# Softcap attention and two feed-forward blocks on one core: sums on fewer or narrower products, and six weight units in plain f32

## The chip, the cores and the metric

The kernel runs on one core of a Trainium2 chip. Its time is the device time of one execution in microseconds; the number for a kernel is the median over several runs. The engines are TensorE (PE in the profile, PEld for its weight loads), VectorE (DVE), ScalarE (ACT), GpSimd (POOL) and SyncE (SP), which issues most DMAs. ScalarE issues some too. TensorE writes into PSUM, the others work between PSUM and SBUF.

## The reference, cut to what matters

```python
def _attn_ref(q, k, v, cap):                 # 4 batches, 12 heads, 448 rows, 64 wide
    scores = 1/sqrt(64) * q @ k^T
    scores = cap * tanh(scores / cap)
    attn = exp(scores - max(scores))
    attn = attn / (sum(attn) + 1e-9)
    return attn @ v

x = attention, heads side by side: (4 * 448, 768)
h = x @ w_in                                 # 768 -> 2048
g = h if h >= 1, 0 if h <= -1, else (h + 1)^2 / 4
y = g @ w_out                                # 2048 -> 768
m = max(y @ w1, y @ w2, y @ w3)              # 768 -> 768
out = m @ w_o2                               # 768 -> 768
```

Everything is f32. The weights arrive as 64-bit words and are turned into f32 on the chip.

## The kernel before

The work is cut by batch (four of 448 tokens) and, in attention, by pairs of heads (six a batch). Tokens lie on the free axis throughout, so the scores of a pair come out transposed, keys on partitions: four chunks of 112 keys, each a tile `t` of 112 x 2 x 448. A row's maximum and sum therefore run across partitions and chunks. For the maximum VectorE joins the four chunks into `mx` and GpSimd reduces over partitions into `mb` (`partition_all_reduce`, L453). VectorE subtracts `mb` from the chunks and ScalarE takes exp.

The sum is taken in one of three ways, by batch. In batch 0 TensorE multiplies each of the four chunks by a 112 x 64 block of ones, for two heads (`total`, L485). In batch 1 it does so with 32 columns of ones and half of the 448 tokens a product, four products side by side a chunk (`total4`, L499). In batches 2 and 3 (`POOLED`) VectorE adds the four chunks into one tile `se` with three additions, and GpSimd reduces it over partitions into `sb` (L534). For all pairs but the last of batch 0, the sums are then gathered by a DMA into a small tile `rc`, turned over there by VectorE, and spread by two more DMAs over a tile `rs`; for the last pair VectorE takes reciprocals of the full tile. Meanwhile TensorE weighs `v` with the chunks into `ps_a` (L619). `xf` is `ps_a` times `rs`.

The feed-forward layers need more precision than a single pass of the type fp32r gives. Each operand is split into a high part and the rest: a copy to fp32r (ScalarE or VectorE) and a subtraction (VectorE). A *part* is one 128 x 128 block of weights against one 128 x 448 tile, in three products: high by high, high by rest, rest by high (L667 to L669). Weights come in 64 units of up to six parts: units 0 to 15 are w_in, 16 to 39 w_out, 40 to 57 w1 to w3, 58 to 63 w_o2. In batch 0 a unit is loaded as 64-bit words (`raw`), converted by VectorE, ScalarE and VectorE (L333, L340, L346) into `wf`, stored to DRAM as f32 and split into `w`; later batches load the stored f32 and split it again. `raw` has three buffers, `wf` and `w` four each.

All operations of the kernel are recorded first, with a due time (`want`), a cost for each engine that can do them, and their tiles. `Plan.run` then places them one by one by due time and by when an engine and a buffer are free, and the engines' programs are emitted in the order that comes out. So a cost or a due time in the table of an operation moves other operations too. Two rules matter here: where two kinds of TensorE work follow each other the plan adds `TURN`, and when GpSimd starts an operation the plan books VectorE for `SHARE` us as well (L136 to L139). The attention of batch b + 1 is spread over the feed-forward pass of batch b; that of batch 0 comes first, with nothing beside it.

```python
    SHARE = 1.4
    FOURS, POOLED = (1,), (2, 3)
    ep = op({"P": 2.95}, reduce_sum, begin + 10 + 7 * gap, [sm], [se], [sb])
    PART, SCORE, STEP, SUM = 0.609, 0.8, 0.755, 0.39
```

Of the kernel before, what the change touches and what calls it, by code (L numbers as in the profile page):

```python
# [14 lines left out]
ALU = mybir.AluOpType  # L15
# [5 lines left out]
class Plan:  # L21
# [43 lines left out]
    def run(self):  # L65
# [39 lines left out]
        while left:  # L105
            moved = True
            while moved:
# [9 lines left out]
                for o in ready:  # L117
# [16 lines left out]
                        c += self.TURN if o.kind != last else 0.0  # L134
                        last = o.kind
                    if e == "P":  # L136
                        free_at["D"] = max(free_at["D"], t) + self.SHARE
                        heapq.heappush(events, (free_at["D"], serial, None))
                        serial += 1  # L139
                    if e == "Q":  # L140
# [54 lines left out]
def kernel(  # L195
# [23 lines left out]
    NF = w_in.shape[0]  # L219
    NM = w123.shape[1]  # L220
    WU = w_in.shape[2]
    FOURS, POOLED = (1,), (2, 3)

    def pool(name, bufs, **kw):
        return ctx.enter_context(tc.tile_pool(name=name, bufs=bufs, **kw))
# [144 lines left out]
    def weights(b, i, want):  # L370

        n = width[i]
        wf, got = (fetch_first if b == 0 else fetch_again)(i, want)
        w = buf("w", "w", [P, 2, WU], F32R)
        hi = op(
            c_copy(n / 1000),
            lambda e: copy(e, w.tile[:, 0, :n], wf.tile[:, :n]),
            want - 9, [got], [wf], [w],
        )
        lo = op(  # L380
            c_tt(n / 1000),
            lambda e: tt(
                e, w.tile[:, 1, :n], wf.tile[:, :n], f32(w.tile[:, 0, :n]), ALU.subtract
            ),
            want - 8, [got, hi], [wf, w],
        )
        return w, [hi, lo]


    def attention(b, i, begin, last):  # L390
# [113 lines left out]
            return fn  # L504

        w = begin + 9 + 6 * gap
        if fours or first:
            g = Group(NCH)
            sums = [
                op({"T": SUM if fours else STEP}, (total4 if fours else total)(t[c], g),  # L510
                   w + 0.1 * c, [exps[c]], [t[c], pr], [pr] if c == 0 else [],
                   "sums" if fours else "columns")
                for c in range(NCH)
            ]
            for c in range(1, NCH):
                sums[c].deps.append(sums[0])
        else:
            se = unit("se", rows=C)
            sm = op(
                c_tt(2 * KS),  # L520
                lambda e: tt(e, se.tile, t[0].tile, t[1].tile, ALU.add),
                w, exps[:2], [t[0], t[1]], [se],
            )
            for c in range(2, NCH):
                sm = op(
                    c_tt(2 * KS),
                    lambda e, c=c: tt(e, se.tile, se.tile, t[c].tile, ALU.add),
                    w + 0.1, [sm, exps[c]], [se, t[c]],
                )
            if pooled:  # L530
                sb = unit("sb", rows=C)

                def reduce_sum(e):
                    nc.gpsimd.partition_all_reduce(  # L534
                        out_ap=sb.tile.rearrange("p h s -> p (h s)"),
                        in_ap=se.tile.rearrange("p h s -> p (h s)"),
                        channels=C, reduce_op=bass.bass_isa.ReduceOp.add,
                    )

                ep = op({"P": 2.95}, reduce_sum, begin + 10 + 7 * gap, [sm], [se], [sb])  # L540
            else:
                sums = [op(
                    {"T": STEP}, total(se, Group(1)), begin + 10.9 + 8 * gap, [sm], [se],
                    [pr], "columns",
                )]
        w = begin + 10 + 8.2 * gap

        cols = S // 2 if fours else S
# [14 lines left out]
        if small:  # L563
# [5 lines left out]
            def gather(e):  # L569
                if pooled:  # L570
                    src = sb.tile[0:1].rearrange("p h (c q) -> p (h c) q", q=C)
                else:
                    step = 32 if fours else D
                    src = rs.tile[0:P:step, :cols].rearrange("p (c q) -> p c q", q=C)
                nc.scalar.dma_start(out=rc.tile, in_=src)

            def spread(e):
                nc.sync.dma_start(out=back, in_=rc.tile)
# [6 lines left out]
                    )  # L585

            src = sb if pooled else rs
            r = op({"A": 0.6}, gather, w + 0.05, [ep], [src], [rc])
            r = op({"S": 3.0 if first else 5.0}, lambda e: None, w + 0.06, [r], [rc, src])

            def turn_over(e):
# [23 lines left out]
        def weigh(c):  # L615
# [10 lines left out]


        avs = [op(
            {"T": STEP}, weigh(0), w, [vl] + (exps[:1] if first else exps + ([] if pooled else sums)),
            [t[0], vt], [pa], "columns",  # L630
        )]
        for c in range(1, NCH):
# [15 lines left out]
            lambda e: tt(e, x.tile[:, 1], xf.tile, f32(x.tile[:, 0]), ALU.subtract),  # L648
            w + 1, [a, hi], [xf, x],
        )  # L650
        return x, [hi, lo]


    def sl(m):
# [1 line left out]

    def parts(pos, want, w, srcs, first, count, ps, g, take):

        wt, wops = w
        done = []  # L660
        for j in range(count):
            a, aops = srcs[first + j]

            def fn(e, j=j, a=a):
                start, stop = g.flags()
                wh, wl = wt.tile[:, 0][:, sl(j)], wt.tile[:, 1][:, sl(j)]
                nc.tensor.matmul(ps.tile[:, :S], wh, a.tile[:, 0], start=start, stop=False)  # L667
                nc.tensor.matmul(ps.tile[:, :S], wh, a.tile[:, 1], start=False, stop=False)  # L668
                nc.tensor.matmul(ps.tile[:, :S], wl, a.tile[:, 0], start=False, stop=stop)  # L669

            o = op(
                {"T": PART}, fn, want(pos + j), [*aops, *wops], [wt, a, ps],
                [ps] if take and j == 0 else [], "layer",
            )
            done.append(o)
        return done
# [176 lines left out]
```

## Time and profile before

| what | us or share |
|---|---|
| median of 3 runs | 1052.28 (1052.06 to 1053.23) |
| profiled execution / its span | 1049.13 / 1047.3 |
| TensorE busy | 1027.1 (98%), 5472 records |
| VectorE busy | 812.3 (78%) |
| ScalarE busy | 508.2 (49%) |
| GpSimd busy | 154.2 (15%), 36 reductions |
| HBM read and written | 131.89 and 27.61 MB |

The busy shares over the span, in 40 slices of 26 us (each digit in tenths, 9 is 90% or more):

```
PE   7988999999999999999999999999999999999998
DVE  5999999898994889868877589777788578655552
ACT  6887996674571856423523377525235144200101
POOL 2321012011010122132222031231221200000000
DMA  7339879889885332444234423335432432234331
```

The first three slices are the attention of batch 0. Then come four feed-forward passes of some 240 us each, the last without attention beside it and so shorter. A product with f32 operands is shown as two records, since it is issued in two; an fp32r product is one record. Products are pipelined: the duration shown of one overlaps the next, and the time that one takes out of TensorE is read from start to start. The page's time of the profiled execution is that of one execution; the median comes from others.

### The profile page before, as it was taken

Reading aid. Unit: us, or ns where it says so; the run is one execution under the profiler, and the core shown is the slowest. Engines: PE = TensorE matmul, PEld = TensorE weight load, DVE = VectorE, ACT = ScalarE, POOL = GpSimd, SP = SyncE. Lnnn points to the kernel's source line nnn. Section 1 sums busy time; section 2 is a strip of 40 time slices with the busy share of each in tenths; the row PEclk is TensorE's granted clock in tenths of the full one; section 3 lists DMA queues with packets and bytes.
Section 4 is the critical chain, followed back from the end, with each engine's and each line's share of the span. In section 5 each row is a group of like instructions: output and inputs, shape, how many; then the busy total and the mean of one; then the engine's idle time right before and its main releaser. Section 6 shows DMA issues by size and latency. Waiting matters only on the chain.

```text
span 1047.3 us, 14331 instructions
## 1 busy us (share of the span) xinstructions
PE 1027.1 (98%) x5472; PEld 813.3 (78%) x5472; DVE 812.3 (78%) x1066; ACT 508.2 (49%) x738; POOL 154.2 (15%) x40
## 2 busy tenths in 40 slices
PE   7988999999999999999999999999999999999998
PEld 2237787787888878878877888788788799999997
DVE  5999999898994889868877589777788578655552
ACT  6887996674571856423523377525235144200101
POOL 2321012011010122132222031231221200000000
PEclk9999999999999999999999999999999999999999
DMA  7339879889885332444234423335432432234331
GB/s 162 123 105 295 280 226 295 290 299 302 285 290 187 99 116 68 119 136 148 96 106 132 146 91 92 108 99 157 126 107 84 143 117 95 91 115 136 106 106 53
DMA packets 66783, 160.53 MB, mean 153 GB/s; under 512 B 8218, under 2 KB 25754, under 8 KB 66714
## 3 DMA queue, kind: packets, MB, share of 16 engines
q1 hardware_dynamic: 66256, 159.53, 48.2%
q8 instruction: 43, 0.70, 0.3%
q14 instruction: 26, 0.21, 0.1%
q10 hardware_dynamic: 458, 0.08, 0.0%
HBM read 131.89 MB, written 27.61 MB: 152 GB/s over the span
## 4 chain that ended last, share of the span: by engine, by line
PE 79%; DVE 7%; DMA 4%; ACT 3%; issue 3%; POOL 3%; SPq 1%; ACTq 0%; POOLq 0%; DVEq 0%
PE ps_m L667 23%; PE ps_m L669 22%; PE ps_m L668 22%; PE ps_s L425 5%; PE ps_a L619 5%; DVE t L257 2%; POOL mb L453 2%; POOL sb L534 1%; DVE mx L257 1%; DMA qk<-in_qk 1%; DVE w L257 1%; PE ps_r L499 1%; ACT t L471 1%; DVE h L750 1%; DMA wf<-w 1%
## 5 line engine op out<-in xcount | busy, mean ns | idle before, releaser
L257 DVE TENSOR_TENSOR w<-wf,w 128x768 fp32r<-128x768 f32 (+1 forms) x256 | 257.1, 1006 | 8.1 <-ACT w L252 4.5
L667 PE MATMUL ps_m<-y,w 128*128 128x448 f32 x432 | 160.4, 371 | 0.0
L254 DVE CAST w<-wf 128x768 fp32r<-128x768 f32 (+1 forms) x120 | 62.5, 521 | 125.2 <-PE ps_m L669 118.7
L668 PE MATMUL ps_m<-y,w 128*128 128x448 f32 x432 | 158.3, 366 | 0.0
L669 PE MATMUL ps_m<-y,w 128*128 128x448 f32 x432 | 158.3, 366 | 0.0
L453 POOL PARTITION_ALL_REDUCE mb<-mx x24 | 79.3, 3306 | 532.7 <-DVE mx L257 424.0
L669 PE MATMUL ps_m<-x,w 128*128 128x448 f32 x384 | 141.4, 368 | 2.9 <-DVE w L257 2.9
L252 ACT ACTIVATE w<-wf 128x768 fp32r<-128x768 f32 (+1 forms) x136 | 101.9, 752 | 86.3 <-PE ps_m L669 60.7
L667 PE MATMUL ps_m<-x,w 128*128 128x448 f32 x384 | 142.8, 372 | 0.0
L667 PE MATMUL ps_m<-g,w 128*128 128x448 f32 x384 | 142.5, 371 | 0.0
L668 PE MATMUL ps_m<-x,w 128*128 128x448 f32 x384 | 141.1, 367 | 0.0
L669 PE MATMUL ps_m<-g,w 128*128 128x448 f32 x384 | 140.5, 366 | 0.0
L668 PE MATMUL ps_m<-g,w 128*128 128x448 f32 x384 | 140.5, 366 | 0.0
L432 ACT ACTIVATE t<-ps_s,qscale 112x896 f32<-112x896 f32 x96 | 92.2, 1003 | 41.9 <-PE ps_s L425 41.9
L471 ACT ACTIVATE t<-t,cap_sb 112x896 f32<-112x896 f32 x96 | 96.5, 1037 | 23.8 <-DVE t L257 23.5
L257 DVE TENSOR_TENSOR t<-t,mb 112x896 f32<-112x896 f32 x96 | 100.1, 1080 | 6.7 <-POOL mb L453 6.7
L667 PEld LDWEIGHTS ps_m<-y,w 128*128 128x128 f32 x432 | 81.1, 188 | 20.3 <-issue 13.4
L425 PE MATMUL ps_s<-qk 64*48 64x448 f32 (+1 forms) x768 | 88.1, 562 | 6.8 <-DMA qk<-in_qk 4.5
L534 POOL PARTITION_ALL_REDUCE sb<-se x12 | 74.7, 6223 | 130.6 <-DVE se L257 118.4
L667 PEld LDWEIGHTS ps_m<-g,w 128*128 128x128 f32 x384 | 72.1, 188 | 18.8 <-issue 10.6
L669 PEld LDWEIGHTS ps_m<-y,w 128*128 128x128 f32 x432 | 81.1, 188 | 7.1
L668 PEld LDWEIGHTS ps_m<-y,w 128*128 128x128 f32 x432 | 81.2, 188 | 6.9
(60 smaller groups left out, 1464.5 us busy)
## 6 DMA issues: line engine op xcount, KB each, us to landing
wf<-w SPq DMA_DIRECT2D x120, 384.0 KB
wf<-w SPq DMA_DIRECT2D x72, 256.0 KB
w<-wf SPq DMA_DIRECT2D x40, 384.0 KB
raw<-in_w SPq DMA_DIRECT2D x18, 768.0 KB
raw<-in_w_in SPq DMA_DIRECT2D x16, 768.0 KB
raw<-in_w_out SPq DMA_DIRECT2D x24, 512.0 KB
qk<-in_qk SPq DMA_DIRECT2D x48, 224.0 KB
w<-wf SPq DMA_DIRECT2D x24, 256.0 KB
```

What stands on the lines that cost most here:

```text
L252: nc.scalar.activation(out=out_, in_=in_, func=AF.Copy)
L254: nc.vector.tensor_copy(out_, in_)
L257: nc.vector.tensor_tensor(out=out_, in0=a, in1=b, op=o)
L425: nc.tensor.matmul(ps.tile[k : k + n, j, :S], qkt.tile[o, 1, c * C + k : c * C + k + n], qkt.tile[o, 0], start=True, stop=True,)
L432: nc.scalar.activation(out=t[c].tile, in_=ps.tile[:C, :, :S], func=AF.Tanh, scale=qscale[:C])
L453: nc.gpsimd.partition_all_reduce(out_ap=mb.tile.rearrange("p h s -> p (h s)"), in_ap=mx.tile.rearrange("p h s -> p (h s)"), channels=C, re ...
L471: lambda e, c=c: nc.scalar.activation(out=t[c].tile, in_=t[c].tile, func=AF.Exp, scale=cap_sb[:C]),
L534: nc.gpsimd.partition_all_reduce(out_ap=sb.tile.rearrange("p h s -> p (h s)"), in_ap=se.tile.rearrange("p h s -> p (h s)"), channels=C, re ...
L619: nc.tensor.matmul(pa.tile[j * D : (j + 1) * D, :S], vt.tile[:, j, c], t[c].tile[:, j], start=start, stop=stop,)
L667: nc.tensor.matmul(ps.tile[:, :S], wh, a.tile[:, 0], start=start, stop=False)
L668: nc.tensor.matmul(ps.tile[:, :S], wh, a.tile[:, 1], start=False, stop=False)
L669: nc.tensor.matmul(ps.tile[:, :S], wl, a.tile[:, 0], start=False, stop=stop)
```

## The change

Four things are changed.

1. The sums of batch 0 (all pairs but the last) are taken by `total4`, as four products of 32 columns side by side a chunk, instead of two of 64.
2. In batch 1 VectorE first adds the chunks in twos (`se` of chunks 0 and 1, `se` of 2 and 3), and TensorE sums two tiles a pair instead of four. They fall due later than before, next to the weighing products.
3. For batches 2 and 3 the plan's cost of GpSimd's sum goes from 2.95 to 6.1, and the time booked on VectorE beside a GpSimd operation grows with that operation's cost (1.4 for 3 us). The DMA that gathers these sums is issued by SyncE instead of ScalarE.
4. The first six units of w_in are not split in batch 0: their parts are one f32 product each, of `wf` and `xf`.

```diff
-                        free_at["D"] = max(free_at["D"], t) + self.SHARE
+                        free_at["D"] = max(free_at["D"], t) + self.SHARE * c / 3
...
-    FOURS, POOLED = (1,), (2, 3)
+    PLAIN = 6
+    ADDED, FOURS, POOLED = (0, 2, 3, 3), (0, 1), (2, 3)
...
         wf, got = (fetch_first if b == 0 else fetch_again)(i, want)
+        if b == 0 and i < PLAIN:
+            return wf, [got], True
         w = buf("w", "w", [P, 2, WU], F32R)
...
-        return w, [hi, lo]
+        return w, [hi, lo], False
...
+        if ADDED[b] == 0:
+            srcs = list(zip(t, exps))
+        elif ADDED[b] == 2:
+            srcs = []
+            for c in (0, 2):
+                se = unit("se", rows=C)
+                srcs.append((se, add(t[c], t[c + 1], se, w, exps[c : c + 2])))
         else:
             se = unit("se", rows=C)
+            sm = add(t[0], t[1], se, w, exps[:2])
             for c in range(2, NCH):
+                sm = add(se, t[c], se, w + 0.1, [sm, exps[c]])
+            srcs = [(se, sm)]
...
-                ep = op({"P": 2.95}, reduce_sum, begin + 10 + 7 * gap, [sm], [se], [sb])
+            ep = op({"P": 6.1}, reduce_sum, begin + 10 + 7 * gap, [sm], [se], [sb])
+        else:
+            g = Group(len(srcs))
+            sums = [
+                op({"T": SUM if fours else STEP}, (total4 if fours else total)(x, g),
+                   (w if first else begin + 10.9 + 8 * gap) + 0.1 * c, [d], [x, pr],
+                   [pr] if c == 0 else [], "sums" if fours else "columns")
+                for c, (x, d) in enumerate(srcs)
+            ]
...
-                nc.scalar.dma_start(out=rc.tile, in_=src)
+                (nc.sync if pooled else nc.scalar).dma_start(out=rc.tile, in_=src)
...
-            r = op({"A": 0.6}, gather, w + 0.05, [ep], [src], [rc])
+            r = op({"Q": 0.1} if pooled else {"A": 0.6}, gather, w + 0.05, [ep], [src], [rc])
...
+            if plain:
+                a, aop = srcs[first + j][2:]
+                aops = [aop]
...
+                if plain:
+                    nc.tensor.matmul(
+                        ps.tile[:, :S], wt.tile[:, sl(j)], a.tile, start=start, stop=stop
+                    )
+                    return
...
-                {"T": PART}, fn, want(pos + j), [*aops, *wops], [wt, a, ps],
-                [ps] if take and j == 0 else [], "layer",
+                {"T": 0.755 if plain else PART}, fn, want(pos + j), [*aops, *wops],
+                [wt, a, ps], [ps] if take and j == 0 else [], "plain" if plain else "layer",
```

What this does to the engines' orders is shown at three places. In the rows, `x_...` and `xf_...` are tiles of batch 0's six pairs, and numbers tell buffers apart; they are other numbers after than before.

Order A, TensorE, from the last pair of batch 0's attention (`ps_r`, `ps_a`) into the first layer (`ps_m`). Before:

```order
L485 MATMUL ps_r_660<-t_577,ones_90 64x448 x2
L619 MATMUL ps_a_665<-t_577,v_489 64x448 x2
L667 MATMUL ps_m_699<-x_451,w_650 128x448
L668 MATMUL ps_m_699<-x_451,w_650 128x448
L669 MATMUL ps_m_699<-x_451,w_650 128x448
L667 MATMUL ps_m_699<-x_522,w_650 128x448
```

After:

```order
L677 MATMUL ps_m_695<-xf_562,wf_683 128x448
L490 MATMUL ps_r_700<-t_543,ones_90 64x448 x2
L625 MATMUL ps_a_705<-t_543,v_513 64x448 x2
L490 MATMUL ps_r_700<-t_574,ones_90 64x448 x2
L625 MATMUL ps_a_705<-t_574,v_513 64x448 x2
L677 MATMUL ps_m_695<-xf_637,wf_683 128x448
L677 MATMUL ps_m_695<-xf_691,wf_683 128x448
L677 MATMUL ps_m_749<-xf_482,wf_718 128x448
L677 MATMUL ps_m_695<-xf_747,wf_683 128x448
```

Each part is one product now; two of them (the first of unit 0, with `xf_482`, stands four rows above) come among pair 5's products, and after those come three parts that need no late `xf`, then one with pair 4's (`xf_747`), two more of unit 1, and the one with pair 5's.

Order B, TensorE, the sums (`ps_r`) and weighing products (`ps_a`) of batch 1's first pair, in units 5 to 7. Before:

```order
L499 MATMUL ps_r_949<-t_580,ones_90 32x224 x4
L499 MATMUL ps_r_949<-t_608,ones_90 32x224 x4
L499 MATMUL ps_r_949<-t_622,ones_90 32x224 x4
...
L499 MATMUL ps_r_949<-t_635,ones_90 32x224 x4
...
L619 MATMUL ps_a_1046<-t_580,v_569 64x448 x2
```

After:

```order
L504 MATMUL ps_r_964<-se_923,ones_90 32x224 x4
L504 MATMUL ps_r_964<-se_933,ones_90 32x224 x4
L625 MATMUL ps_a_982<-t_600,v_615 64x448 x2
L625 MATMUL ps_a_982<-t_623,v_615 64x448 x2
L625 MATMUL ps_a_982<-t_625,v_615 64x448 x2
L625 MATMUL ps_a_982<-t_633,v_615 64x448 x2
```

The sums are half as many and stand right ahead of the weighing products, with no layer product between.

Order C, VectorE, at the end of w1 to w3 in batch 1: `se` are the additions for GpSimd's sum of batch 2's last pair, `top` the maximum over the three layers' PSUM tiles, `w` a weight unit's second half, `m` the second half of the last tile of the next layer's input. Before:

```order
L257 TENSOR_TENSOR se_4938<-t_4806,t_4814 112x896
L257 TENSOR_TENSOR top_4918<-ps_m_4910,top_4918 128x448
L257 TENSOR_TENSOR se_4938<-se_4938,t_4831 112x896
L257 TENSOR_TENSOR se_4938<-se_4938,t_4836 112x896
L257 TENSOR_TENSOR w_4946<-wf_4809,w_4946 128x768
L257 TENSOR_TENSOR top_4918<-ps_m_4942,top_4918 128x448
L257 TENSOR_TENSOR w_4973<-wf_4874,w_4973 128x768
L257 TENSOR_TENSOR m_4988<-top_4918,m_4988 128x448
```

After:

```order
L260 TENSOR_TENSOR se_4855<-t_4727,t_4732 112x896
L260 TENSOR_TENSOR top_4841<-ps_m_4831,top_4841 128x448
L260 TENSOR_TENSOR se_4855<-se_4855,t_4752 112x896
L260 TENSOR_TENSOR w_4866<-wf_4695,w_4866 128x768
L260 TENSOR_TENSOR se_4855<-se_4855,t_4757 112x896
L260 TENSOR_TENSOR top_4841<-ps_m_4861,top_4841 128x448
L260 TENSOR_TENSOR w_4877<-wf_4720,w_4877 128x768
L260 TENSOR_TENSOR m_4904<-top_4841,m_4904 128x448
```

The third addition and the first `w` have changed places. On TensorE the part that needs this `m` is the tenth of its layer after and the seventh before. Batch 2 has the same rows at the same place.

## Rows read from the trace of the kernel before

**Rows 1.** Stages: us, busy us (instructions) of PE, PEld, DVE, ACT, POOL, clock, DMA, GB/s.

```profile
60.00:84.00 24.00, 18.79 (x96) 8.59 (x93) 23.86 (x31) 16.91 (x22) 3.01 (x1) 0.97 0.52 166
84.00:314.00 230.00, 229.23 (x1306) 181.17 (x1308) 212.55 (x305) 165.85 (x241) 21.56 (x6) 1.00 0.87 284
```

**Rows 2.** Timeline of TensorE: start, us, engine, line, op, tiles, records [idle before].

```profile
73.45 0.92 PE L485 MATMUL ps_r<-t,ones 112*64 112x448 f32 x4
74.20 0.92 PE L619 MATMUL ps_a<-t,v 112*64 112x448 f32 x4
...
76.79 0.47 PE L667 MATMUL ps_m<-x,w 128*128 128x448 f32 x1
...
82.10 0.53 PE L669 MATMUL ps_m<-x,w 128*128 128x448 f32 x1 [2.21 <-DVE w L257]
82.42 0.57 PE L667 MATMUL ps_m<-x,w 128*128 128x448 f32 x1
82.80 0.57 PE L668 MATMUL ps_m<-x,w 128*128 128x448 f32 x1
...
103.49 0.37 PE L668 MATMUL ps_m<-x,w 128*128 128x448 f32 x1
103.69 0.37 PE L669 MATMUL ps_m<-x,w 128*128 128x448 f32 x1
103.99 1.72 PE L425 MATMUL ps_s<-qk 64*64 64x448 f32 x16
105.64 1.65 PE L499 MATMUL ps_r<-t,ones 112*32 112x224 f32 x24
107.22 0.47 PE L667 MATMUL ps_m<-x,w 128*128 128x448 f32 x1
```

**Rows 3.** Timeline of VectorE at the end of batch 0's attention.

```profile
74.80 0.54 DVE L333 TENSOR_SCALAR raw<-raw 128x768 int32<-128x768 uint32 x1
...
76.13 0.95 DVE L346 SCALAR_TENSOR_TENSOR wf<-raw 128x768 int32<-128x768 int32 x1
77.01 2.97 DVE L607 RECIPROCAL rs<-rs 128x112 f32<-128x112 f32 x4
80.08 0.62 DVE L257 TENSOR_TENSOR xf<-ps_a,rs 128x448 f32<-128x448 f32 x1
80.62 0.55 DVE L333 TENSOR_SCALAR raw<-raw 128x768 int32<-128x768 uint32 x1
...
81.96 0.62 DVE L257 TENSOR_TENSOR xf<-ps_a,rs 128x448 f32<-128x448 f32 x1
```

**Rows 4.** Chain of waits: start, us from start to start, the sums of batch 1.

```profile
108.70 0.52 PE ps_r L499 x8
...
146.74 0.89 PE ps_r L499 x16
...
188.88 1.65 PE ps_r L499 x32
```

**Rows 5.** Tile se: duration in ns (min, median, max), first and last start.

```profile
L257 DVE TENSOR_TENSOR se<-t x12: 1080/1084/1085, 359.8 to 807.8; 112x896 f32<-112x896 f32 x12
```

**Rows 6.** What TensorE waited for, 84 to 320 us: total, times, longest.

```profile
PE ps_m L669 <- DVE w L257: 0.7, 1, 0.7
```

**Rows 7.** Timelines of VectorE, GpSimd and TensorE, start of batch 1's last layer.

```profile
558.25 0.62 DVE L257 TENSOR_TENSOR top<-ps_m,top 128x448 f32<-128x448 f32 x1
...
561.85 0.62 DVE L257 TENSOR_TENSOR top<-ps_m,top 128x448 f32<-128x448 f32 x1
562.61 3.96 DVE L257 TENSOR_TENSOR w<-wf,w 128x768 fp32r<-128x768 f32 x1
...
561.22 5.96 POOL L534 PARTITION_ALL_REDUCE sb<-se  x1 [10.83 <-DVE se L257]
...
565.21 0.37 PE L667 MATMUL ps_m<-m,w 128*128 128x448 f32 x1
567.16 0.47 PE L668 MATMUL ps_m<-m,w 128*128 128x448 f32 x1 [1.59 <-DVE m L257]
```

More of the change, by code (lines that the diff above doesn't have):

```diff
@@ L506, in attention, with add @@
         w = begin + 9 + 6 * gap
[L507 to L516, printed above, removed]
+        def add(x, y, out, w, deps):
+            return op(
+                c_tt(2 * KS), lambda e: tt(e, out.tile, x.tile, y.tile, ALU.add),
+                w, deps, [x, y, out], [] if out is x else [out],
+            )
@@ L517, in attention @@
+        if ADDED[b] == 0:
[5 more added lines that the diff above has]
+                srcs.append((se, add(t[c], t[c + 1], se, w, exps[c : c + 2])))
         else:
             se = unit("se", rows=C)
[L519 to L523, printed above, removed]
@@ L524, in attention @@
-            for c in range(2, NCH):
[L525 to L528, printed above, removed]
-                )
[L530 to L538, printed above, removed]
-                ep = op({"P": 2.95}, reduce_sum, begin + 10 + 7 * gap, [sm], [se], [sb])
[L541 to L545, printed above, removed]
+            sm = add(t[0], t[1], se, w, exps[:2])
@@ new lines, in attention, with reduce_sum @@
+            for c in range(2, NCH):
+                sm = add(se, t[c], se, w + 0.1, [sm, exps[c]])
+            srcs = [(se, sm)]
+        if pooled:
+            sb = unit("sb", rows=C)
+            def reduce_sum(e):
+                nc.gpsimd.partition_all_reduce(
+                    out_ap=sb.tile.rearrange("p h s -> p (h s)"),
+                    in_ap=se.tile.rearrange("p h s -> p (h s)"),
+                    channels=C, reduce_op=bass.bass_isa.ReduceOp.add,
+                )
+            ep = op({"P": 6.1}, reduce_sum, begin + 10 + 7 * gap, [sm], [se], [sb])
[7 more added lines that the diff above has]
+            ]
+            for c in range(1, len(srcs)):
+                sums[c].deps.append(sums[0])
@@ L628, in attention @@
         avs = [op(
-            {"T": STEP}, weigh(0), w, [vl] + (exps[:1] if first else exps + ([] if pooled else sums)),
+            {"T": STEP}, weigh(0), w,
+            [vl] + (exps[:1] if first else exps if pooled else exps + sums),
             [t[0], vt], [pa], "columns",
@@ L650, in attention @@
         )
-        return x, [hi, lo]
+        return x, [hi, lo], xf, a
     def sl(m):
@@ L657, in parts @@
     def parts(pos, want, w, srcs, first, count, ps, g, take):
-        wt, wops = w
+        wt, wops, plain = w
         done = []
         for j in range(count):
-            a, aops = srcs[first + j]
+            a, aops = srcs[first + j][:2]
+            if plain:
+                a, aop = srcs[first + j][2:]
+                aops = [aop]
             def fn(e, j=j, a=a):
                 start, stop = g.flags()
+                if plain:
+                    nc.tensor.matmul(
+                        ps.tile[:, :S], wt.tile[:, sl(j)], a.tile, start=start, stop=stop
+                    )
+                    return
                 wh, wl = wt.tile[:, 0][:, sl(j)], wt.tile[:, 1][:, sl(j)]
```

## The prediction

> **What bounds the kernel now.** I read the table of stages first. From 84 to 314 us, which is most of the feed-forward pass of batch 0 beside the attention of batch 1, TensorE is busy for 229.2 of 230 us, VectorE for 212.6, and the DMA engines for 0.87 of the time [rows 1]. The reader is to see that TensorE sets the end there, and that VectorE has only 17.4 us to spare. From 60 to 84 us, the last pairs of batch 0's attention, it is the other way round: VectorE is busy for 23.9 of 24 us and TensorE for 18.8. In the later batches VectorE has more slack (the table of shares by slice in the section on the profile). So work taken from TensorE counts after about 77 us, and work taken from VectorE counts before that. The timeline of TensorE then shows where it loses time: it begins the first layer at 76.79, stands until 82.10 for a second half on VectorE (2.2 us), and then takes products 0.38 apart (82.42 to 82.80) where 0.20 is usual (103.49 to 103.69) [rows 2]: the granted clock is at its 1.2 GHz level for a few us, as the mean of 0.97 says [rows 1]. After 104 us its only long waits are two, of 1.6 us each, at the start of the last layer in batches 1 and 2; the first is shown [rows 7].
>
> **The start, up to the end of weight unit 5.** Six units are 36 parts. Before they are 108 products from 76.79 to 103.99: 27.2 us, of which 108 x 0.203 = 21.9 is work and 5.3 is waiting and the slow clock [rows 2]. After, each part is one f32 product over 448 columns. The trace has no f32 product of 128x128, so its price is bounded from both sides. The f32 products of the sums and of attention take 0.75 for two that run side by side (73.45 to 74.20) [rows 2]; the three products that it replaces take 0.61, and four single passes would take 4 x 0.203 = 0.81. I take 0.75, the same type over the same number of columns.
> What starts them is xf of the last two pairs. On VectorE the stretch up to 74.80 keeps its order, with one cast of 0.3 more. Behind it stand now raw, wf, raw, wf, four reciprocals, and xf, x, xf: at 0.54, 0.88 (76.13 to 77.01), 3.07 (77.01 to 80.08) and 0.54 (80.08 to 80.62) that is 74.8 + 0.3 + 2.84 + 3.07 + 1.62 = 82.6; before, the second xf ends at the same 82.6 (81.96 and 0.62) [rows 3]. Two subtractions left, a conversion and the second half of one x came in. By then eight of the 36 plain parts are done (order A: two beside pair 5's sums, six while xf is awaited). The other 28 end at 82.6 + 28 x 0.75 = 103.6, against 104.0: **-0.4**. That units 0 to 5 need no split gains little, since xf ends when it did: the 5.3 us of waiting pay for 36 x 0.14 = 5.0 of dearer products. Bounds: at 0.81 a product 1.7 more; if the clock falls again, ten products or so at twice the time, 1.8 more (the ten of before); if VectorE ends xf one us earlier, 1 less. SyncE's queue now has unit 4's load behind the spreading of pair 4's reciprocals; VectorE wants it after 82.6, so 0, and inside the bounds if late. Four 32-column products a chunk for batch 0's sums save TensorE some 0.75 x 2 a pair, but before 77 us, beside a full VectorE: nothing. The smaller eps there is on ScalarE, which has 7 us idle in that stage [rows 1].
>
> The Trainium skill (FP8 and Floating Point Precision, TensorE Precision Notes) counts four passes for true FP32. At this trace's 0.203 for a single pass that is 0.81, while its f32 rows of the same length show 0.75 [rows 2]. By the rule the forecast would be 1.7 us later.
>
> **The sums of batch 1.** Before, 16 products of 32 columns a pair: 1.65 in one piece (four pairs), twice 0.89 in two pieces, and once 1.58 (105.64 to 107.22) and 0.52 [rows 2, 4]; 10.5 for six pairs. After, eight products, as in the piece of 0.89: 5.3. They now stand right ahead of the weighing products (order B), so that TensorE changes between kinds of work 112 times instead of 120 from the first layer on; a change costs 0.1 (103.69 to 103.99 against 0.20) [rows 2]. Together 5.2 + 0.8: **-6.0**. All of it lies in stages where TensorE is full. Bounds: -5.2 without the changes, -6.5.
>
> The two additions a pair cost VectorE 12 x 1.08 = 13.0 us [rows 5], beside 17.4 of slack in that stage [rows 1]. The plain units take six subtractions off it, most of them ahead of 100 us, and its order has 22 casts and copies fewer, 16 of which go to ScalarE, with 64 us to spare there [rows 1]. In sum it fits, with not much room. Cost on the path between 0 and 13.0. I take **+1.0**, near the lower end: at 92% busy VectorE held TensorE up for only 0.7 us between 84 and 320 us [rows 6].
>
> **GpSimd's sums.** At the start of the last layer in batch 1 GpSimd's sum runs from 561.22 for 5.96 us. VectorE's subtraction of two SBUF tiles at 562.61 takes 3.96 and ends 5.35 after GpSimd's start; the second half of m stands behind it, and TensorE goes on at 567.16, having begun the product ahead at 565.21 [rows 7]. The op between, which reads PSUM (561.85), isn't held. Batch 2 repeats it. The planner now books 2.85 us for this instead of 1.4, and the order changes in two places. On VectorE (order C) the third addition stands behind w, so that GpSimd starts later: 558.25 + 0.54 for top, two additions at 1.02 and w at 0.87 by their starts, and 0.24 as before: 561.9; the hold ends at 567.3, m at 567.8. And TensorE has three more parts before the product that needs m, nine instead of six, so it gets there at 565.4 + 9 x 0.207 = 567.3. It waits 0.6 instead of 1.6, twice: **-2.0**. Bounds: -3.2 (no wait) and +2.0 (the addition one us later still and the three parts not ready).
> The gather that SyncE issues now waits in its queue ahead of weight loads until GpSimd is done; the loads go into four wf buffers and lead by several us, so 0, and +1 if one comes late. On ScalarE the copies that stood behind the gather are free: nothing, TensorE didn't wait for them.
>
> The Trainium skill (SBUF — State Buffer, SBUF: two separate sides) says that the shared port pair is held for the whole instruction. Here the hold ends 0.6 before GpSimd's recorded end [rows 7]. By the rule m would come 0.6 later at both places, 1.2 us on the forecast.
>
> **The sum.** -0.4 - 6.0 + 1.0 - 2.0 = -7.4. The profiled execution took 1049.1 us, 1.8 of them around its span of 1047.3, and is 3.2 below the median of the runs; the difference is carried over: 1052.3 - 7.4 = 1044.9.
>
> **Rivals.**
> - VectorE becomes the bound in batch 0 (slower). Place: the weights' second halves between 110 and 314 us. The 13.0 us of additions reach TensorE in full from the point where the lead of the four w buffers is used up: -0.4 - 6.0 - 2.0 + 13.0 = +4.6: 1056.9. For it: 92% busy, and DMA at 0.87 leaves little to catch up with. Against: casts can move to ScalarE, and 17.4 is more than 13.0.
> - Start and GpSimd's sums give nothing: products at 0.81, a second fall of the clock, the waits for m as before: -0.4 + 1.7 + 1.8 - 6.0 + 1.0 = -1.9: 1050.4. For it: the clock fell here after long waits of TensorE. Against: they are shorter now.
> - The second half of m comes later still, since GpSimd starts later: +2.0 in place of -2.0: 1048.9. For it: w and m both stand behind the hold. Against: three more parts of cover.
> - The full hold, by the mechanism above: 1046.1; the hold shown ends early.
> - TensorE's saved products turn into idle time: 1052.3.
>
> **How the numbers follow.** Forecast case 0.66 (1041 to 1048), m later 0.09, start and sums nothing 0.10, full hold 0.03, idle 0.05, VectorE bound 0.07. The range 1041.0 to 1050.5 has the sum of the low bounds (-0.4 - 1 + 0 - 6.5 - 3.2 = -11.1) at its low end and the second rival at its high end. A measurement of this kernel tells 0.2% from no change, 2.1 us, so faster means below 1050.2: forecast, m later, full hold and half of the second rival, 0.83; within, 0.10; slower 0.07.
>
> **What would show it.** Right: plain products 0.75 apart and unit 6 beginning at 103.6; the sums at 0.9 a pair, six times; a wait for m under 1 us in batches 1 and 2; no wait for w between 110 and 314 us. Wrong: if the granted clock falls during the plain parts, if a plain product takes over 0.8, or if TensorE waits for VectorE's w by over 3 us in batch 0.

## The result, and the profile after

The changed kernel takes 1042.15 us (median of 6 runs, 1041.43 to 1043.38) beside 1052.01 for the kernel before (6 runs, 1049.29 to 1053.23): ratio 0.9913, 95% interval 0.9899 to 0.9926: 9.1 us faster by the ratio, 9.9 by the medians. A second set of runs gave 1042.25 beside 1050.04, ratio 0.9917 (0.9898 to 0.9936). The forecast was 1044.9.

The profiled execution of after took 1043.38 (span 1041.6), the longest of its six; that of before, 1049.13, lay below all six timed runs of that kernel. So the two traces differ by only 5.7 us, and the medians by more. The stages of after, to be held against [rows 1]:

```profile
60.00:84.00 24.00, 19.24 (x93) 5.97 (x90) 19.19 (x23) 11.67 (x15) 3.00 (x1) 0.86 0.37 110
84.00:314.00 230.00, 229.76 (x1199) 175.54 (x1198) 217.77 (x306) 171.15 (x250) 20.69 (x6) 1.00 0.89 290
```

From 84 to 314 us TensorE is as full as before and VectorE fuller (217.8 against 212.6). The surprise is the first row: at the end of batch 0's attention VectorE, full before, is idle for 4.8 of 24 us, and the granted clock is 0.86 instead of 0.97. TensorE's timeline shows where it begins; idle time stands in brackets with what ended it:

```profile
59.18 0.97 PE L430 MATMUL ps_s<-qk 64*64 64x448 f32 x8 [0.39 <-ACT t L437]
62.22 0.58 PE L504 MATMUL ps_r<-t,ones 112*32 112x224 f32 x8 [2.07 <-ACT t L476]
62.73 3.09 PE L625 MATMUL ps_a<-t,v 112*64 112x448 f32 x8
...
66.92 1.72 PE L625 MATMUL ps_a<-t,v 112*64 112x448 f32 x8
...
72.02 0.97 PE L490 MATMUL ps_r<-t,ones 112*64 112x448 f32 x4 [1.83 <-ACT t L476]
...
87.21 21.31 PE L677 MATMUL ps_m<-xf,wf 128*128 128x448 f32 x56 [0.24 <-DVE xf L260]
108.01 0.71 PE L682 MATMUL ps_m<-x,w 128*128 128x448 f32 x1
```

After standing for 2.07 us TensorE takes 3.09 for eight records of weighing products that take 1.72 a little later: the granted clock is at its 1.2 GHz level, from 62.9 to 66.3. It falls again at 73.2, behind the wait of 1.83, and once at 49.3 (3.4 us each). Before, the trace had one such fall, at 82.4, behind the wait of 2.21 in [rows 2]. What the slow products delay is read on ScalarE and VectorE:

```profile
69.22 0.36 ACT L559 ACTIVATE rs<-ps_r 128x224 f32<-128x224 f32 x1 [2.85 <-PE ps_r L504]
69.61 0.53 ACTq L581 DMA_DIRECT2D rc<-rs  x1
```

```profile
75.24 0.84 DVE L602 RECIPROCAL rc<-rc 8x112 f32<-8x112 f32 x1 [2.81 <-DMA rc<-rs]
...
83.83 0.56 DVE L260 TENSOR_TENSOR xf<-ps_a,rs 128x448 f32<-128x448 f32 x1
86.53 0.62 DVE L260 TENSOR_TENSOR xf<-ps_a,rs 128x448 f32<-128x448 f32 x1
```

The small copy behind the sums waits 2.85 for them, the gather leaves at 69.61, and VectorE, in order, stands 2.81 for its landing. (In a version without these falls, the long waits filled, below, the copy waits 1.87 and VectorE not at all.) The last xf begins at 86.53, where [rows 3] had 81.96, and weight unit 6 at 108.01, where the same point was 103.99 before [rows 2].

Behind that, the places that the prediction named are as forecast or better. TensorE's only wait from 84 us to the end is the 0.2 for xf above. A pair's sums in batch 1 are one piece of eight products, 0.90 from start to start, against [rows 4]:

```profile
115.14 0.96 PE L504 MATMUL ps_r<-se,ones 112*32 112x224 f32 x16
116.04 3.23 PE L625 MATMUL ps_a<-t,v 112*64 112x448 f32 x16
```

And the place of [rows 7], VectorE and GpSimd, then TensorE:

```profile
558.79 0.62 DVE L260 TENSOR_TENSOR top<-ps_m,top 128x448 f32<-128x448 f32 x1 [0.23 <-PE ps_m L684]
559.33 4.20 DVE L260 TENSOR_TENSOR w<-wf,w 128x768 fp32r<-128x768 f32 x1
563.46 0.61 DVE L260 TENSOR_TENSOR m<-top,m 128x448 fp32r<-128x448 f32 x1
...
558.76 5.39 POOL L535 PARTITION_ALL_REDUCE sb<-se  x1 [11.24 <-PE ps_m L684]
```

```profile
564.17 0.37 PE L682 MATMUL ps_m<-m,w 128*128 128x448 f32 x1
564.38 0.37 PE L683 MATMUL ps_m<-m,w 128*128 128x448 f32 x1
```

The subtraction w, of two SBUF tiles, is held as before (4.20 us), but m is there at 564.1 and TensorE's product that needs it comes after nine parts, at 564.4: no wait. GpSimd's sum, which also goes from one SBUF tile to another, takes 5.39 instead of 5.96. Before, it started while VectorE was at a subtraction of two SBUF tiles, of which this is the row ([rows 7] has the rows behind it):

```profile
560.98 0.95 DVE L257 TENSOR_TENSOR w<-wf,w 128x768 fp32r<-128x768 f32 x1
```

After, it starts 0.03 ahead of `top`, which reads PSUM. The other sums of the two traces bear this out: where a w is under way at the start and a PSUM read and the next w follow, the sum takes 5.95 to 5.97 (eight of them), and where no operation of two SBUF tiles is under way, 5.39 or 5.40 (six).

### The profile page after: what moved, and what is told of

Same layout as the page of the kernel before. It is cut to its first block, busy times and chain, and to the rows that moved or that the text cites. A ratio compares the mean times of both kernels' runs of the same rounds, so it can differ in the third digit from the quotient of the medians.

```text
span 1041.6 us, 14247 instructions
## 1 busy us (share of the span) xinstructions
PE 1023.3 (98%) x5420; PEld 801.8 (77%) x5420; DVE 807.2 (77%) x1050; ACT 517.9 (50%) x754; POOL 149.6 (14%) x40
## 4 chain that ended last, share of the span: by engine, by line
PE 94%; ACT 3%; DVE 1%; DMA 1%; issue 0%; ACTq 0%; DVEq 0%
PE ps_m L682 27%; PE ps_m L683 26%; PE ps_m L684 26%; PE ps_s L430 7%; PE ps_a L625 7%; PE ps_m L677 2%; ACT t L437 2%; PE ps_r L504 1%; ACT t L476 1%; DMA rc<-rs 1%; DMA qk<-in_qk 0%; DVE rs L613 0%; DVE wf L349 0%; ACTq L581 0%; DVE t L260 0%
## 5 line engine op out<-in xcount | busy, mean ns | idle before, releaser
L260 DVE TENSOR_TENSOR w<-wf,w 128x768 fp32r<-128x768 f32 (+1 forms) x250 | 244.0, 978 | 5.9 <-ACT w L255 2.8
L257 DVE CAST w<-wf 128x768 fp32r<-128x768 f32 (+1 forms) x110 | 57.6, 524 | 137.7 <-PE ps_m L684 133.4
L255 ACT ACTIVATE w<-wf 128x768 fp32r<-128x768 f32 (+1 forms) x140 | 105.3, 755 | 98.6 <-PE ps_m L684 79.8
L682 PE MATMUL ps_m<-x,w 128*128 128x448 f32 x348 | 129.2, 371 | 0.0
L684 PE MATMUL ps_m<-x,w 128*128 128x448 f32 x348 | 127.3, 366 | 0.0
L683 PE MATMUL ps_m<-x,w 128*128 128x448 f32 x348 | 127.3, 366 | 0.0
L535 POOL PARTITION_ALL_REDUCE sb<-se x12 | 70.7, 5895 | 138.7 <-DVE se L260 59.0
```

The costliest lines, as they stand in the source:

```text
L255: nc.scalar.activation(out=out_, in_=in_, func=AF.Copy)
L257: nc.vector.tensor_copy(out_, in_)
L260: nc.vector.tensor_tensor(out=out_, in0=a, in1=b, op=o)
L535: nc.gpsimd.partition_all_reduce(out_ap=sb.tile.rearrange("p h s -> p (h s)"), in_ap=se.tile.rearrange("p h s -> p (h s)"), channels=C, re ...
```

## The experiments

All are timed beside the kernel before on the same chip; its median was 1049.2 to 1050.0 in these sets. "The start" is when unit 6 begins in the profiled execution. The sets ran on three chips, so medians of different sets are compared with care. First, parts were taken out of the changed kernel one at a time (the move of the gather to SyncE was not).

**Batch 0's sums wide again.**

```
-    ADDED, FOURS, POOLED = (0, 2, 3, 3), (0, 1), (2, 3)
+    ADDED, FOURS, POOLED = (0, 2, 3, 3), (1,), (2, 3)
```

> The changed kernel with batch 0's sums as before (products of 64 columns that leave the sums in all rows), all else kept. Theory A: the narrow sums are what makes the start late. They take TensorE less time in batch 0's attention, so it idles more there, and the granted clock falls to its 1.2 GHz level three times instead of once. With the wide sums one fall at most, weight unit 6 begins at about 104 us instead of 108.0, and the time is about 4 below the changed kernel's 1042.2: 1038.2. Rival B: the start is late for another reason (the order of VectorE with the plain units, a late DMA for the reciprocals): unit 6 still at 107 to 108 and 1041 to 1043.

Measured: 1038.96 (1038.08 to 1040.81), ratio 0.9901 (0.9885 to 0.9917). The mean granted clock was 1.000 in all five executions, and the profiled one has no fall before its last microsecond; unit 6 begins at 103.27. Its stage and TensorE's waits there:

```profile
60.00:84.00 24.00, 22.76 (x100) 7.78 (x97) 23.72 (x31) 15.58 (x20) 3.13 (x1) 1.00 0.52 170
```

```profile
59.70 0.97 PE L490 MATMUL ps_r<-t,ones 112*64 112x448 f32 x4 [0.29 <-ACT t L476]
...
70.20 0.97 PE L490 MATMUL ps_r<-t,ones 112*64 112x448 f32 x4 [1.21 <-ACT t L476]
```

The two waits of 2.07 and 1.83 are 0.29 and 1.21 here, the clock stays at 2.4 GHz and VectorE is busy for 23.7 of 24 us. The narrow sums cost the changed kernel 3.3 us by the medians (no run of the one reaches into those of the other; the ratios' intervals overlap). That they do it by giving TensorE less to do is not shown by this.

**No plain units.**

```
-    PLAIN = 6
+    PLAIN = 0
```

> The changed kernel without plain units (units 0 to 5 split into two halves, three products a part). Theory A: the falls of the clock stay (two or three before 84 us), unit 6 begins at 107.5 to 109.5, the time is within 1.5 of the changed kernel: 1041 to 1043.5. Rival B: the plain units' order is the cause: unit 6 at about 104, one fall of the clock, 1038.

Measured: 1049.60 (1046.01 to 1054.98), ratio 0.9996 (0.9977 to 1.0014). Both theories were wrong on the size: without the plain units 7.4 us of the gain are gone. What TensorE waited for from 84 to 314 us (total, times, longest) has a part of the reason:

```profile
PE ps_m L684 <- DVE w L260: 5.2, 5, 1.4
```

These are the five, the last of 0.2 left out, and VectorE's first addition for batch 1:

```profile
86.17 0.47 PE L684 MATMUL ps_m<-x,w 128*128 128x448 f32 x1 [1.27 <-DVE w L260]
...
99.76 0.47 PE L684 MATMUL ps_m<-x,w 128*128 128x448 f32 x1 [1.43 <-DVE w L260]
...
110.33 0.47 PE L684 MATMUL ps_m<-x,w 128*128 128x448 f32 x1 [1.14 <-DVE w L260]
...
153.04 0.47 PE L684 MATMUL ps_m<-x,w 128*128 128x448 f32 x1 [1.21 <-DVE w L260]
```

```profile
114.88 2.08 DVE L260 TENSOR_TENSOR se<-t 112x896 f32<-112x896 f32 x2
```

Three of them, 3.8 us, end before any addition of batch 1: with six more subtractions early in batch 0, VectorE is late with second halves by itself, as in the kernel before at 82.10 [rows 2]. Only the other 1.4 of waiting stands behind an addition. Unit 5's last product begins at 106.56, and the clock falls twice, as in the changed kernel's second profiled execution below (1042.03, unit 6 at 106.47). From there to batch 1's first layer the layers' own products take 4.6 more than in that one (191.3 against 186.7), of which 2.5 are waits; so most of the difference of 5.3 between the two profiled executions stands there. The median is higher still: the three executions with the lowest mean clock, 0.993, took 1051.3 to 1055.0.

**The planner's old price for GpSimd's sums**, with SyncE's gather kept.

```
-                        free_at["D"] = max(free_at["D"], t) + self.SHARE * c / 3
+                        free_at["D"] = max(free_at["D"], t) + self.SHARE
...
-            ep = op({"P": 6.1}, reduce_sum, begin + 10 + 7 * gap, [sm], [se], [sb])
+            ep = op({"P": 2.95}, reduce_sum, begin + 10 + 7 * gap, [sm], [se], [sb])
```

> The changed kernel with the planner's old price for GpSimd's sums (2.95 us, a constant share for VectorE); the gather stays on SyncE. Theory A: the price alone takes away the waits of TensorE for m at the last layer of batches 1 and 2, so they come back with 1.6 us each and the time is 3.2 above the changed kernel: 1045.4. Rival B: the waits went because SyncE's gather freed ScalarE, not by the price: no waits, 1042.

Measured: 1044.70 (1044.29 to 1046.49), ratio 0.9957, 2.5 above the changed kernel. The waits, 314 to 840 us:

```profile
PE ps_m L683 <- DVE m L260: 3.2, 2, 1.6
```

The waits are theory A's: the planner's price takes them away, and the gather on SyncE alone does not. (The price with the old gather was not run.) The time is 0.7 below what A gave.

**No additions in batch 1.**

```
-    ADDED, FOURS, POOLED = (0, 2, 3, 3), (0, 1), (2, 3)
+    ADDED, FOURS, POOLED = (0, 0, 3, 3), (0, 1), (2, 3)
```

> The changed kernel with four chunks a pair to sum in batch 1 instead of two pairs of chunks added on VectorE. Theory A: the additions cost nothing on the path, so the time is higher by the 48 products that come back and the changes of kind, 5.2 to 6.0 us: 1047.4 to 1048.2, and VectorE is busy for some 205 of 230 us between 84 and 314. Rival B: the additions hold TensorE up by part of what they save: under 4 us higher, 1042 to 1046.

Measured: 1048.81 (1047.80 to 1050.73), ratio 0.9991, 6.6 above the changed kernel; VectorE is busy for 207.4 of 230. Rival B falls: with the plain units no cost of the additions shows on the path. The time lies 0.6 above theory A's range. From unit 6 to the end of batch 0 the sums take 4.5 us more and the layers' own products 1.9 more (188.4 against 186.5), and for the second figure the theory had only the changes of kind.

Then the cause of the late start.

**The changed kernel again.**

> The changed kernel itself again, beside the other kernels of this set, since times moved by 0.2% between sets: 0.9913 of the kernel before, 1040.6 if that takes 1049.7. Two or three falls of the granted clock before 84 us, unit 6 at 106 to 108.

Measured: 1042.25 (1041.60 to 1042.93), ratio 0.9917. Falls at 61.4 and 71.7, unit 6 at 106.47: with two falls the start is 1.5 earlier than with the three of the first profiled execution.

**The lost work given back to TensorE.** Four products a chunk against a tile of zeros, same order.

```
+                for i in range(4 if first else 0):
+                    o = slice(i % 2 * (S // 2), (i % 2 + 1) * (S // 2))
+                    nc.tensor.matmul(
+                        pr.tile[i * 32 : (i + 1) * 32, : S // 2], zeros[:, :32],
+                        src.tile[:, i // 2, o], start=False, stop=stop,
+                    )
```

> The changed kernel with four more products of 32 columns a chunk in batch 0's sums, against a tile of zeros and added to the same sums: the same numbers, the same order and the same narrow copies behind them, but TensorE as long at work on these sums as with the wide ones. Theory A: the idler TensorE is what makes the clock fall: with the added work at most one fall, unit 6 at 103 to 105, and 2 to 4 below the changed kernel although TensorE does more. Rival B: the other order of the narrow sums or their narrow copies delay the pairs: falls as before, unit 6 at 107 to 110, and the time is the same or 1 to 3 above the changed kernel.

Measured: 1047.16 (1046.12 to 1048.88), ratio 0.9965. Theory A falls, and the time and unit 6 lie beyond rival B's ranges too. TensorE is busy for 37.1 of 40 us from 20 to 60, nearly as with wide sums (37.7), and yet:

```profile
65.93 0.98 PE L506 MATMUL ps_r<-t,ones 112*32 112x224 f32 x8 [2.07 <-ACT t L478]
66.67 0.97 PE L512 MATMUL ps_r<-t,zeros 112*32 112x224 f32 x8
67.58 3.26 PE L633 MATMUL ps_a<-t,v 112*64 112x448 f32 x8
```

The same wait of 2.07 in one piece stands at the same place of the order, and the clock falls, here at 65.4, half a us before the wait ends, and for 6.8 us; unit 6 begins at 111.6. So how much TensorE does in the stage as a whole isn't what decides.

**The plain units alone, on the kernel before.** The code of the plain parts as in the change, and of the rest what stood before.

```
+    PLAIN = 6
...
+        if b == 0 and i < PLAIN:
+            return wf, [got], True
```

> The kernel before with six plain units and nothing else. Theory A: the prediction's term for the plain units holds when the clock doesn't fall, -0.4, and the one or two falls of the kernel before go as well (1.7 each): ratio 0.996 to 0.9985, no fall before 110 us. Rival B: the plain units are what the changed kernel gains most from (without them it gains nothing): -7 to -9, ratio 0.992.

Measured: 1049.85 (1046.44 to 1051.33), ratio 0.9985 (0.9971 to 0.9999). The ratio is at the upper end of theory A's; its sign, no fall, failed in the profiled execution. There is one fall, at 70.3 behind a wait of 1.81, and unit 5's last product begins at 103.7, no earlier than before. Four of the twelve executions had a mean clock of 1.000; they took 1046.4 to 1050.7, so the falls are not all that makes the executions differ.

**The narrow sums of batch 0 alone, on the kernel before.**

```
-    FOURS, POOLED = (1,), (2, 3)
+    FOURS, POOLED = (0, 1), (2, 3)
```

> The kernel before with batch 0's sums as products of 32 columns and nothing else. Theory A: TensorE is idler in batch 0's attention, three falls of the clock or more before 90 us, the start is 3 to 9 later, ratio 1.003 to 1.009. Rival B: neutral, as the prediction had it: ratio 0.999 to 1.001.

Measured: 1051.78 (1050.50 to 1057.34), ratio 1.0016 (0.9999 to 1.0032). Three falls (50.8, 71.3, 84.9). The falls are A's and the ratio lies between the two theories; its interval takes in no change.

**Narrow sums in an order like that of the wide ones.** The planner books them as "columns" at 0.755 us a chunk.

```
-                op({"T": SUM if fours else STEP}, (total4 if fours else total)(x, g),
+                op({"T": SUM if fours and not first else STEP}, (total4 if fours else total)(x, g),
...
-                   [pr] if c == 0 else [], "sums" if fours else "columns")
+                   [pr] if c == 0 else [], "sums" if fours and not first else "columns")
```

> The changed kernel, where the planner treats batch 0's narrow sums as it treats wide ones (the same kind of work as the weighing products, and 0.755 us a chunk), so that they alternate with the weighing products and the scores as before, while the products themselves stay narrow and short. Theory B (the order: in blocks behind each other, TensorE stands twice for 2 us in one piece for an exponential, and the clock falls right after): such waits go down to 1.2 or less, at most one fall, unit 6 at 103 to 105, 1038 to 1040. Theory A (TensorE has less to do, whatever the order): two or three falls as in the changed kernel, unit 6 at 106 or later, 1041 to 1043.

Measured: 1039.88 (1038.57 to 1041.22), ratio 0.9906 (0.9889 to 0.9923). One fall left, at 69.3, right at the end of the one long wait that is left (2.94, to 69.10); unit 6 at 104.12. In time and start it is theory B's; of the waits only the first is shorter (1.31), the second is longer than in the changed kernel (1.83).

**The long waits filled.** The changed kernel, its order kept, with two products that nobody reads ahead of the first sum of pairs 4 and 5.

```
+        def filler(start):
+            for _ in range(2 if start and first and i >= 4 else 0):
+                nc.tensor.matmul(
+                    pr.tile[:D, :S], ones, vt.tile.rearrange("p a c d -> p (a c d)")[:, :S],
+                    start=True, stop=True,
+                )
```

> The changed kernel, with two f32 products over 448 columns (of v, into the sums' own place, overwritten by the sums) ahead of the first sum of the last two pairs of batch 0, where TensorE stood for 2.07 and 1.83 us and the granted clock fell right behind. They take some 1.5 us, so nothing has to be later, and the order of all else is kept. Theory A: TensorE's standing there is what the falls follow; with 0.3 to 0.6 us left of the two waits no fall between 58 and 80 us, unit 6 at 103 to 105 instead of 106.5, time 1038.5 to 1040.5. Rival B: the falls come from the stage's load as a whole, or of the order on the other engines: falls as before, unit 6 at 106 to 108, 1041.5 to 1043.

Measured: 1039.56 (1039.05 to 1041.50), ratio 0.9913 (0.9899 to 0.9926; before had 1049.21 in this set). TensorE's timeline there, then the same place in the changed kernel's second profiled execution, and the stage of this kernel:

```profile
58.79 1.72 PE L488 MATMUL ps_r<-v,ones 112*64 112x448 f32 x4
60.93 0.59 PE L513 MATMUL ps_r<-t,ones 112*32 112x224 f32 x8 [0.42 <-ACT t L476]
61.44 1.85 PE L634 MATMUL ps_a<-t,v 112*64 112x448 f32 x8
```

```profile
60.76 0.59 PE L504 MATMUL ps_r<-t,ones 112*32 112x224 f32 x8 [2.07 <-ACT t L476]
61.28 3.15 PE L625 MATMUL ps_a<-t,v 112*64 112x448 f32 x8
```

```profile
60.00:84.00 24.00, 21.85 (x104) 7.19 (x103) 23.08 (x30) 12.25 (x16) 3.00 (x1) 1.00 0.48 149
```

There is no fall in this stage of the profiled execution, the weighing products take 1.85 instead of 3.15, VectorE is busy for 23.1 of 24 us and no longer waits for the gathered sums, and unit 6 begins at 104.03 instead of 106.47. Four useless products are worth 2.7 us by the medians; the ratios to before (0.9913 and 0.9917) don't tell this apart. The executions do: three of five had a mean clock of 1.000 (1039.05 to 1039.56) and two 0.998 (1041.28 and 1041.50), while the changed kernel's twelve had 0.995 to 0.997. That TensorE's standing at these two places brings the clock down, and with it most of the late start, is shown by this; the 0.8 that is left against the wide sums (103.27) is not explained.

Two tries at more, both on the version with wide sums. **Three additions a pair in batch 1:**

```
-    ADDED, FOURS, POOLED = (0, 2, 3, 3), (0, 1), (2, 3)
+    ADDED, FOURS, POOLED = (0, 3, 3, 3), (1,), (2, 3)
```

> Batch 0's sums wide as before, and in batch 1 all four chunks added on VectorE (three additions a pair), so that one chunk is left for TensorE to sum: 24 products of 32 columns fewer than with two additions, 2.7 us, for 6.5 us more of VectorE. Theory A: VectorE has room for it from 110 to 314 us (it was held to 190 of 204): 2 to 2.7 below the kernel with wide sums in batch 0 (1039.0), 1036.5. Rival: VectorE is now the bound, TensorE waits for w there by 3 us or more: 1039 to 1043.

Measured: 1040.93 (1039.09 to 1044.78), ratio 0.9923. The time is in the rival's range, but not by its mechanism. VectorE does have room: it is busy for 222.3 of 230 us and TensorE waits for no w. In the profiled executions batch 0's last layer begins 2.6 us earlier than with two additions (304.25 against 306.87), as expected. The gain is given back later: in that layer the split products come 205.1 ns apart instead of 202.7 on the mean, in batch 1's first 206.1 instead of 203.1, in its second 205.7 instead of 204.6 (the three layers take 0.47, 0.83 and 0.29 us longer), and batch 3's first layer is 0.8 longer. At the end 0.2 is left. The medians, of two sets, even put this kernel 2.0 above the wide sums; the traces don't show that, and the ratios' intervals overlap (0.9900 to 0.9946 here).

**Four plain units:**

```
-    PLAIN = 6
+    PLAIN = 4
```

> Batch 0's sums wide as before, and four plain units instead of six. Theory A: the split products of units 4 and 5 save 12 parts x 0.14 = 1.7 us and VectorE has their second halves ready in time: 1037.3. Rival: the second halves are late as in the kernel before, TensorE waits 1 to 3 us for them and the clock may fall: 1039 to 1043.

Measured: 1040.76 (1039.84 to 1044.35), ratio 0.9920. TensorE waits 2.3 for w, in two pieces, and the clock doesn't fall: the rival. Neither shows a gain over the wide sums with six plain units (1038.96), which by the medians beat the changed kernel.

## Why the prediction was right, and where it was wrong

1042.15 lies 2.7 below the forecast and within its range, but that it came so near is in part luck: an error of 4.4 in the start and one of 4.4 in what was carried over from the median cancel, as the sums below show. Of the signs that it named, the plain products' pitch, the sums at 0.9, no wait for m and none for w came; unit 6 at 103.6 did not. By its steps, in the two profiled executions:

- **Start, -0.4.** Wrong: +4.0 (108.0 against 104.0). The plain product's price was right (0.755 a product: 55 records, two to a product, in 20.77 us from 87.21). The 0.81 that four passes at 0.203 would take didn't come: 0.755 is four times 0.189. With wide sums the term comes out as forecast, -0.7 (103.27). The step that failed is the one that cost batch 0's narrow sums at "nothing". It looked at the sums' busy time and at VectorE as the cover; it didn't ask where in the order they and the weighing products now stand. In blocks of their own they leave TensorE nothing to do while an exponential is awaited: 2.07 us at 60 to 62, where the wide sums left 0.29 (the order by itself, with the sums narrow, 1.31). The second long wait is not theirs alone: it is 1.81 with plain units alone and 1.21 with the wide sums. With the falls, VectorE's stretch "keeps its order" but not its time. The prediction had a second fall of the clock as a bound and a rival; it put it into the plain products, not into the attention.
- **Sums of batch 1, -6.0.** Right for the products: six pieces of 0.90 make 5.4 where 5.3 was forecast, against 10.5 before, so -5.1. The 0.8 for the changes of kind isn't seen by itself; see the sum below. Taking the additions out costs 6.6.
- **VectorE, +1.0.** Mis-sized: it is 0, TensorE waits for no w from 84 us on. The 0.7 of [rows 6] was no measure for it, since it stands in the start's stretch, at 96.77:

```profile
96.77 0.47 PE L669 MATMUL ps_m<-x,w 128*128 128x448 f32 x1 [0.67 <-DVE w L257]
```

  But the reason given, that it fits, leans on the plain units: without them TensorE waits 5.2 for w, 1.4 of it behind batch 1's first addition.
- **GpSimd's sums, -2.0.** Mis-sized: -3.2, no wait left. TensorE has the nine parts, as forecast, and GpSimd starts later against `top`, as forecast; but its sum takes 5.39 instead of the assumed 5.96, so m is there in time. The prediction had seen that w comes ahead of the third addition, and not that GpSimd then starts beside a PSUM read instead of a w. The old price brings 1.6 twice back, and the 5.95.

From that point to the end the two spans are 943.3 (1047.3 - 104.0) and 933.6 (1041.6 - 108.0): -9.7, where the terms were -7.0. Up to batch 1's first layer it is 6.9: 5.1 in the sums and 1.7 in the layers' own products (188.3 to 186.5), which takes in fewer changes of kind and products that come closer together; no wait for VectorE stands there, before or after. Behind that it is 2.9: the last layers of batches 1 and 2 are 3.9 shorter, of which the waits are 3.2, and batch 2's other layers take some 1.0 more. So for its own execution the forecast was 4.4 too low in the start and 2.7 too high behind it: 1041.7 + 4.4 - 2.7 = 1043.4. What hid this in the median is the **carry-over**. The prediction added 3.2, since before's profiled execution lay so far below its median; the one of after lies 1.2 above its own, together 4.4: as much as the start was off. In before, too, the executions differ by how often the clock falls. Of the 67 that were timed beside the experiments, the 11 with a mean clock of 0.995 took 1052.6 on the mean, the 16 with 0.998, as in the profiled one with its single fall, 1049.0; but these go from 1047.1 to 1053.7, so the falls are only a part of it. A stretch whose time depends on such falls is better given a term of its own than left in what is carried over.

The full hold of the rival is not seen. The Trainium skill (SBUF — State Buffer, SBUF: two separate sides) has the shared port pair held for the whole instruction; here w ends at 563.53 and GpSimd's sum at 564.15, 0.62 later, as in [rows 7].

What stays open: why an execution of the same program has two falls or three (the one at 49.3 came beside waits of 1.2 and 0.9, which the second profiled execution has without a fall), and why before's trace has none behind this wait:

```profile
70.36 0.97 PE L485 MATMUL ps_r<-t,ones 112*64 112x448 f32 x4 [2.99 <-ACT t L471]
```

## What to carry to other kernels

Making an engine's work cheaper where it isn't the bound may not be free: look for the longest single stretch in which TensorE then stands, and for the clock behind it. Where there is one, let it do other work there, even useless work, or keep an order that mixes kinds of work. Price the parts of a change together where they use one engine: here the plain units alone were worth 1.5 (0.1 to 3.0), and taken out of the whole change they cost 7.4.

## What the runs showed of the hardware

- **A single wait can be enough.** In the fourteen traces TensorE stands 17 times for 1.8 us or more after the first 30 us. With 16 of these the clock was at 1.2 GHz within 1.5 us of the wait's end, as with 2.07 and 1.83 (the changed kernel, in both profiled executions), 1.81 (plain units alone) and 2.94 (the other order). The one of 2.99 in the kernel before is the exception. Of 25 waits of 1.2 to 1.6 us, two had a fall within 1.8 us of their end (1.23 at 47.5 in the changed kernel, 1.28 at 84.4 in the narrow sums alone). The Trainium skill (TensorE: Matmul & The Clock Gate, HAM oscillation — how this bites in real kernels) describes matmuls that pay for each wait anew with a spell at half the clock; these traces agree but for that exception, and the rows of the changed kernel above show the price paid on other engines too (2.85 us of waiting on ScalarE against 1.87 with the waits filled, 2.81 on VectorE against none).
- **A split product has two pitches.** Eight of them, from start to start, in two layers of the changed kernel:

```profile
113.02 0.36 PE L684 MATMUL ps_m<-x,w 128*128 128x448 f32 x1
...
114.64 0.36 PE L683 MATMUL ps_m<-x,w 128*128 128x448 f32 x1
...
558.59 0.37 PE L682 MATMUL ps_m<-m,w 128*128 128x448 f32 x1
...
560.25 0.37 PE L684 MATMUL ps_m<-m,w 128*128 128x448 f32 x1
```

  That is 1.62 and 1.66 us. Over whole layers the means lie between 202.6 and 206.6 ns. The changed kernel's two profiled executions agree in them layer by layer to within 0.7 ns, and from batch 1 on the kernels that differ from it in batch 0's attention alone (lost work given back, long waits filled) agree with it to 0.1, so the pitch goes with the program more than with the execution. The change moved it both ways: batch 0's first layer, from unit 6 on, from 205.8 to 202.7, batch 2's first from 203.3 to 205.9. Its cause wasn't looked for; 3 ns over the 288 products of a first layer are 0.9 us, a third of what three additions a pair had won.
